# Hedgehog linear attention and a Mish dense layer, twice: averages of two row blocks in one visit, transposes between the row tiles, and the last sums in single banks

## The chip, the core and the metric

The kernel runs on one core of a Trainium2 chip. The core has five engines with an instruction queue each: TensorE (PE; its weight loads are shown apart as PEld), VectorE (DVE), ScalarE (ACT), GpSimd (POOL) and SyncE (SP), which here issues the DMAs. Matmuls write to PSUM, here used as eight banks of 128 partitions x 512 fp32. The metric is the time of the program on the device in microseconds, and lower is better. All engines start together, and the program ends when the last store has landed.

## The reference

Two layers. Each is a linear attention with a learned feature map, followed by a dense layer with the Mish activation; both are behind a layer norm without weights and are added to their input. There are 2048 rows of 640 numbers, 32 heads of 20, and 1536 hidden units.

```python
def _A_ref(x, wqkv, w_phi, wo):
    q, k, v = ...                       # x @ wqkv, split into heads of 20
    pq = jnp.einsum("bhsd,hdf->bhsf", q, w_phi)
    pk = jnp.einsum("bhsd,hdf->bhsf", k, w_phi)
    phi_q = jnp.concatenate([_softmax(pq), _softmax(-pq)], axis=-1)
    phi_k = jnp.concatenate([_softmax(pk), _softmax(-pk)], axis=-1)
    kv = jnp.einsum("bhsf,bhsd->bhfd", phi_k, v)
    z = jnp.einsum("bhsf->bhf", phi_k)
    num = jnp.einsum("bhqf,bhfd->bhqd", phi_q, kv)
    den = jnp.einsum("bhqf,bhf->bhq", phi_q, z)[..., None] + 1e-6
    return (num / den) @ wo             # heads put side by side first

def _B_ref(x, w1, b1, w2):
    h = x @ w1 + b1
    return (h * jnp.tanh(softplus(h))) @ w2

x = A_x
for _ in range(2):
    x = x + _A_ref(_layernorm(x), A_wqkv, A_w_phi, A_wo)
    x = x + _B_ref(_layernorm(x), B_w1, B_b1, B_w2)
```

## The kernel before

**Blocks and stages.** The rows are cut into eight blocks of 256, and a block into two row tiles of 128, called 0 and 1. A layer has three stages, each a loop over the blocks. The first attention stage makes the queries' and keys' features and values, sums `kv` and `z` over all rows, and stores the queries' features, turned, in DRAM (`e_d`). The second attention stage divides, multiplies by `wo`, and adds the rows of x. The dense stage does the rest.

**Products in parts.** A product of fp32 operands is made from three: both operands are split into a high part, which the matmul takes whole, and the low rest, and high x high, high x low and low x high are summed in PSUM. So the product of one row tile with a 640 x 320 half of `wo` (`project_half`, L391) is 5 chunks x 3 = 15 matmuls of 320 columns. This document calls one of them a projection.

**The second attention stage (`attend_second`).** For each block and row tile:

- `load(b)` (L646 to L647) brings a block's query features back from `e_d` in three DMAs: two into `big` tiles (a pool of 5) and one into an `ol` tile (a pool of 6). They are free again when the averages of that block have read them.
- `average(b, t)` (L676) multiplies them by `kvb`, the masked sums of all heads, in 22 matmuls of 63 columns (L686): 11 groups of heads, and two halves of 64 rows. The profile shows each as two instructions, so an average is 44. They use 120 x 64 of the array at a time, where all others here use 128 x 128. The result lies in a pair of PSUM banks, numerator and denominator side by side. VectorE then adds the epsilon (L695, twice), takes the reciprocal (L696) and multiplies, once for each bank (L699). These five instructions are called a division here; `div[0]` is the last of them. The rows come out in a row tile (`xn`, a pool of 4).
- `Transposed(...).all()` turns the two row tiles of a block: ten transposes of 128 x 128 on TensorE (L325) in three groups, each group into a single bank, from which ScalarE makes the high part (through the helper on L134) and VectorE the low part (L331).
- `Rows.half(c, ps)` is 15 projections into a single bank (L714), VectorE's addition of the rows of x (L716) and half of the statistics (L717); `mean` joins them (L721).
- `norm_scale(b, mvs)` makes the layer norm's scale and shift: GpSimd adds the epsilon (L304) and takes the power -1/2 (L305), and VectorE makes the shift from it (L307, once for each row tile).
- The block's rows are stored, and weights of the dense layer that were fetched a block before are split (`makes`, `fetches`).

Meanwhile the first attention stage's last query tile is still being finished: `rest` has its steps (projections, then the reductions L416 and L419 among others, then exp, L425, L426, the product on GpSimd, the turn and the stores), and `tail()` issues one of them, behind the last division.

**Order.** Before: blocks 0 and 1 are averaged ahead of the loop. In pass 1 and pass 2 of the loop, the averages of block 2 and block 3 come first; in passes 2 to 5, blocks 4 to 7 are averaged behind the transposes. So a visit of TensorE to the averages is one block, two averages or 88 instructions. Each visit stands between matmuls of another shape.

**What sets the order of instructions.** The whole program stands in a scheduled block: an engine's instructions are put in order by a simulated timeline, except where a part is written by hand. In the second attention stage the order of TensorE and of SyncE is the program's own (`manual_schedule`); VectorE, ScalarE and GpSimd are ordered by the scheduler, and `issue_after(i)` keeps an instruction behind i. In the dense stage all engines are the scheduler's.

**Banks.** PSUM is two pools: `mm_tile` gives pairs of banks (two pairs), `one_tile` single banks (four). A pool gives its buffers in turn, and the first instruction that writes to a buffer waits for the last that reads what it held. In a pass of the second attention stage the single banks are asked for by four halves and three groups of transposes; the averages ask for pairs.

**The dense stage.** `hidden` (L809) makes 256 hidden units of a block in a single bank (two groups of 128, 15 matmuls of 256 columns each), `mish` the activation, and `contract` (L851), two steps later, adds their part of the output into two pairs of banks, one for each row tile, over six steps. `end` adds the rows of x (L861 in the last block, else L869) and stores them. In the last block of the last layer the four halves are added one by one; the first row tile is stored whole (L865), and the second in two halves (L863). A pair of banks is one tile, so a reader of one bank waits for the last matmul that writes to either.

Of the kernel before, what the change touches and what calls it, by code (L numbers as in the profile page):

```python
# [11 lines left out]
ALU = mybir.AluOpType  # L12
# [32 lines left out]
def kernel(  # L45
# [620 lines left out]
    def attend_second(x_src, x_dst, acc, fetches, makes, fetch_next, begin_next):  # L666
# [9 lines left out]
        def average(b, t):  # L676

            phs = loaded[b]
            po = mm_tile()
            for g in range(G):  # L680
# [3 lines left out]
                for q in range(2):  # L684
                    s0 = t * P + 64 * q
                    nc.tensor.matmul(  # L686
                        po[64 * q:64 * q + 64, c, GW * j:GW * j + w], phs[g][:n, s0:s0 + 64],
                        kvb[:n, g, :w], start=True, stop=True)
            o = row_tile()
            den = work.tile([P, H], F32, tag="r", name="den", bufs=2)  # L690
            pv = [po[:, c, :(DH + 1) * n].rearrange("p (h d) -> p h d", d=DH + 1)
# [32 lines left out]
        with tc.manual_schedule(engines={mybir.EngineType.PE, mybir.EngineType.SP}):  # L724
# [18 lines left out]
            def averages(b):  # L743
                for t in range(BT):
                    average(b, t)
# [5 lines left out]
            for b in range(NB):  # L751
                if b == NB - 1:
                    ahead.all()
                elif b in (1, 2):
                    averages(b + 1)
                r0, r1 = Rows(b, 0), Rows(b, 1)
# [4 lines left out]
                if b in (1, 2):  # L761
                    phi(b + 3)
                if b == NB - 3:
# [5 lines left out]
                if b < 2:  # L769
                    r1.half(0, one_tile())  # L770
                if b + 1 < NB:
                    nxt = Transposed(rows.pop(b + 1)).all()
                if 2 <= b < NB - 2:
                    averages(b + 2)
                    phi(b + 4)
                if b == 2:
                    tail()
                if b >= 2:
                    r1.half(0, one_tile())
                r1.half(1, one_tile())  # L780
                norm_scale(b, [mv0, r1.mean()])
# [13 lines left out]
    def dense(x_src, x_dst, w1s, w2s, first, last):  # L795
# [41 lines left out]
        def contract(b, pr, ah, al):  # L837
            if pr == 0:
                blocks[b][2] = [mm_tile() for _ in range(BT)]
            pys = blocks[b][2]  # L840
            order = [(t, j) for t in range(BT) for j in range(2)]
            if b == NB - 1 and pr == KF // 2 - 1:
                order = [(t, j) for j in range(2) for t in range(BT)]
            for t, j in order:
                sl = slice(t * P, (t + 1) * P)
                f = 2 * pr + j
                for c in range(2):
                    cs = slice(c * HC, (c + 1) * HC)
                    wh, wl = w2s[f][0][:, cs], w2s[f][1][:, cs]
                    for n, (l, r) in enumerate(((ah, wh), (ah, wl), (al, wh))):  # L850
                        nc.tensor.matmul(pys[t][:, c, :HC], l[:, j, sl], r,  # L851
                                         start=(f == 0 and n == 0), stop=(f == KF - 1 and n == 2))
# [170 lines left out]
```

## Time and profile before

| | us |
|---|---|
| three runs | 1362.43, 1364.81, 1365.24; median 1364.81 |
| profiled execution | 1361.69 |
| its span in the profile | 1359.7 |

The profiled execution is one more run, and all rows of the trace are its own. Its TensorE clock was granted at 0.999 of full speed. By stages, with the busy time of the engines in each stretch of the span (us) and the share of time in which the mean DMA engine was busy:

| stretch, us | what | PE | DVE | ACT | POOL | DMA | GB/s |
|---|---|---|---|---|---|---|---|
| 42 to 252 | first attention stage, layer 0 | 210.0 | 178.9 | 89.5 | 104.7 | 0.43 | 93 |
| 252 to 356 | second attention stage, layer 0 | 104.0 | 77.0 | 27.9 | 41.0 | 0.86 | 277 |
| 356 to 690 | dense stage, layer 0 | 334.0 | 270.8 | 170.7 | 79.0 | 0.42 | 109 |
| 690 to 911 | first attention stage, layer 1 | 220.8 | 180.9 | 83.5 | 120.7 | 0.45 | 97 |
| 911 to 1018 | second attention stage, layer 1 | 106.4 | 78.2 | 29.5 | 42.6 | 0.86 | 273 |
| 1018 to 1343 | dense stage, layer 1, without its end | 325.0 | 236.2 | 151.8 | 61.7 | 0.27 | 74 |

In the rows below, L391 is line 391 of the kernel; `one<-r2h,xth` is what is written and what is read, by the program's names. A row of the timeline has the start of a group in us from the start of the span, its length, engine, line, operation, operands with their shapes, and how many instructions it holds; what stands in brackets is idle time before it and what ended it. Rows of the waits give the sum of a wait, its count and the longest. A row of the windows has the stretch, the busy time of PE, PEld, DVE, ACT, POOL (with counts), then the granted clock, the DMA share and GB/s.

### The profile page before, as it was taken

The page shows a single profiled execution, that of the slowest core. Times are in us where ns is not written, and L with a number is a line of the kernel's source. Part 1 is how long each engine was busy: PE and PEld are TensorE (multiplying, and loading weights), DVE is VectorE, ACT ScalarE, POOL GpSimd, SP SyncE. Part 2 cuts the span into 40 slices and gives each one's busy share as a digit, 9 for nine tenths or more (in the row PEclk, how much of TensorE's full clock was granted, in tenths as well). Part 3 has the DMA queues.
Part 4 walks back from the last instruction along what each step waited for, and adds up shares of the span by engine and source line. Part 5 has one row for each costly group of instructions (what it writes and reads, how often), then busy time and mean ns, then how long its engine had stood idle before and what let it go on. Part 6 is the DMA issues. An engine that isn't in the chain of part 4 may idle for free.

```text
span 1359.7 us, 30969 instructions
## 1 busy us (share of the span) xinstructions
PE 1349.6 (99%) x12896; PEld 1338.2 (98%) x12896; DVE 1057.4 (78%) x1799; ACT 576.0 (42%) x967; POOL 464.0 (34%) x417
## 2 busy tenths in 40 slices
PE   9999999999999999999999999999999999999998
PEld 9999999999999999999999999999999999999998
DVE  5888988876687887778769788779668776676775
ACT  4444344322454545445443334332236444444443
POOL 2355644444222222222225555634351211111111
PEclk9999999999999999999999999999999999999999
DMA  9543443797714442244563534559964221233200
GB/s 338 156 103 79 98 96 81 206 287 274 222 40 98 117 117 69 61 106 100 145 209 81 119 79 91 96 120 289 289 246 125 78 72 39 86 98 97 73 26 20
DMA packets 352629, 174.11 MB, mean 128 GB/s; under 512 B 287449, under 2 KB 324041, under 8 KB 352489
## 3 DMA queue, kind: packets, MB, share of 16 engines
q1 hardware_dynamic: 352489, 172.14, 46.7%
q8 instruction: 101, 1.65, 0.5%
q14 instruction: 39, 0.32, 0.1%
HBM read 106.23 MB, written 65.86 MB: 127 GB/s over the span
## 4 chain that ended last, share of the span: by engine, by line
PE 94%; DVE 3%; POOL 1%; ACT 0%; issue 0%; DVEq 0%; POOLq 0%
PE mm L391 25%; PE mm L851 25%; PE one L809 25%; PE one L391 12%; PE mm L686 3%; PE one L325 2%; PE one L464 2%; DVE r L425 1%; DVE m L416 0%; DVE r L419 0%; POOL big L427 0%; DVE big L417 0%; DVE r1l L276 0%; POOL xtl L331 0%; POOL r L427 0%
## 5 line engine op out<-in xcount | busy, mean ns | idle before, releaser
L851 PE MATMUL mm<-r2h,ol 128*128 128x320 f32 x1280 | 304.8, 309 | 0.0
L835 POOL TENSOR_TENSOR ol<-big,ol 128x512 fp32r<-128x512 f32 (+1 forms) x98 | 131.1, 1338 | 477.2 <-ACT ol L834 419.1
L809 PE MATMUL one<-xtl,r1h 128*128 128x256 f32 x960 | 268.2, 279 | 0.0
L809 PE MATMUL one<-xth,r1l 128*128 128x256 f32 x960 | 268.0, 279 | 0.0
L809 PE MATMUL one<-xth,r1h 128*128 128x256 f32 x960 | 265.9, 279 | 0.0
L851 PEld LDWEIGHTS mm<-r2h,ol 128*128 128x128 f32 x1280 | 219.2, 188 | 0.0
L851 PE MATMUL mm<-r2l,ol 128*128 128x320 f32 x640 | 197.3, 309 | 0.0
L391 PE MATMUL mm<-r1h,xth 128*128 128x304 f32 (+1 forms) x600 | 185.1, 309 | 1.5 <-DVE r1l L276 1.5
L391 PE MATMUL mm<-r1l,xth 128*128 128x304 f32 (+1 forms) x600 | 183.8, 306 | 0.0
L391 PE MATMUL mm<-r1h,xtl 128*128 128x304 f32 (+1 forms) x600 | 183.5, 306 | 0.2 <-POOL xtl L331 0.2
L809 PEld LDWEIGHTS one<-xtl,r1h 128*128 128x128 f32 x960 | 180.4, 188 | 0.0
L809 PEld LDWEIGHTS one<-xth,r1l 128*128 128x128 f32 x960 | 180.4, 188 | 0.0
L809 PEld LDWEIGHTS one<-xth,r1h 128*128 128x128 f32 x960 | 179.6, 188 | 0.0
L824 DVE TENSOR_SCALAR big<-big 128x512 f32<-128x512 f32 (+1 forms) x98 | 56.6, 578 | 110.0 <-ACT big L822 109.8
L851 PEld LDWEIGHTS mm<-r2l,ol 128*128 128x128 f32 x640 | 120.2, 188 | 0.0
L834 ACT ACTIVATE ol<-big 128x512 fp32r<-128x512 f32 (+1 forms) x98 | 60.9, 622 | 137.8 <-DVE big L833 137.8
L826 ACT ACTIVATE big<-big,two 128x512 f32<-128x512 f32 (+1 forms) x98 | 70.1, 716 | 116.0 <-DVE big L825 115.9
L822 ACT ACTIVATE big<-one,b1s 128x256 f32<-128x256 f32 x192 | 80.9, 468 | 88.5 <-PE one L809 88.0
L427 POOL TENSOR_TENSOR r<-r,r 128x1280 f32<-128x1280 f32 x32 | 77.2, 2413 | 119.1 <-DVE r L426 101.6
L391 PEld LDWEIGHTS mm<-r1h,xth 128*128 128x128 f32 x600 | 112.8, 188 | 2.6 <-DVE r1l L276 1.7
L391 PEld LDWEIGHTS mm<-r1h,xtl 128*128 128x128 f32 x600 | 112.8, 188 | 0.4 <-POOL xtl L331 0.4
L391 PEld LDWEIGHTS mm<-r1l,xth 128*128 128x128 f32 x600 | 112.8, 188 | 0.1
(142 smaller groups left out, 3118.0 us busy)
## 6 DMA issues: line engine op xcount, KB each, us to landing
e_d<-r SPq DMA_DIRECT2D x128, 160.0 KB, 4.0
big<-e_d SPq DMA_DIRECT2D x32, 640.0 KB, 7.6
x_d<-xt SPq DMA_DIRECT2D x23, 640.0 KB, 3.8
xt<-x_d SPq DMA_DIRECT2D x22, 640.0 KB, 5.5
n_d<-xn SPq DMA_DIRECT2D x168, 80.0 KB, 2.3
xt<-in_x SPq DMA_DIRECT2D x16, 640.0 KB, 4.4
xn<-x_d SPq DMA_DIRECT2D x28, 320.0 KB, 4.4
v<-n_d SPq DMA_DIRECT2D x30, 256.0 KB, 3.1
```

The lines of the kernel that those rows point to most:

```text
L325: nc.tensor.transpose(ps[:, c, t * P:(t + 1) * P], self.rows[t][:, (c0 + c) * P:(c0 + c + 1) * P], ident)
L391: nc.tensor.matmul(ps[:, :w], a[:, sl], r, start=(k == 0 and n == 0), stop=(k == KD - 1 and n == 2))
L427: nc.gpsimd.tensor_tensor(eg, eg, r.unsqueeze(2).to_broadcast([P, 2 * H, DH]), op=ALU.mult)
L464: nc.tensor.matmul(kva[32 * j:32 * j + DH + 1, 40 * r:40 * r + 40], v[:, (DH + 1) * h:(DH + 1) * (h + 1)], e[:, 40 * h:40 * h + 40], start ...
L686: nc.tensor.matmul(po[64 * q:64 * q + 64, c, GW * j:GW * j + w], phs[g][:n, s0:s0 + 64], kvb[:n, g, :w], start=True, stop=True)
L809: nc.tensor.matmul(ph[:, j, :], l, r, start=(n == 0), stop=(n == 3 * KD - 1))
L822: exps[0] = nc.scalar.activation(part(ta, 0)[:, j - js.start], ph[:, j, :], AF.Exp, bias=b1s[:, 2 * pr + j:2 * pr + j + 1]).ins
L824: nc.vector.tensor_scalar_min(e, e, E_CAP)
L826: nc.scalar.activation(r, n, AF.Ln, bias=two)
L834: nc.scalar.activation(ah[:, js], n, AF.Copy)
L835: nc.gpsimd.tensor_tensor(al[:, js], n, ah[:, js].bitcast(F32), op=ALU.subtract)
L851: nc.tensor.matmul(pys[t][:, c, :HC], l[:, j, sl], r, start=(f == 0 and n == 0), stop=(f == KF - 1 and n == 2))
```

## The change

Second attention stage:

- `averages(b)` now does the four averages of blocks b and b+1 in a row. They stand at the start of passes 1, 3 and 5, and there alone: blocks 2 and 3, 4 and 5, 6 and 7. The first two and the fourth have a pair of banks, and the third has two single banks (`single`).
- The loads follow: passes 1 and 3 issue those of two blocks each, 4 and 5, 6 and 7.
- In passes 0, 2 and 4, `norm_scale` is moved to the next pass, behind the averages, and behind their last division by `issue_after(div[0])`.
- The transposes of the next block now always stand between row tile 0 and row tile 1. Before, in passes 0 and 1, the first half of row tile 1 came ahead of them.

End of the last layer:

- In the last block, row tile 1's sums have two single banks in place of a pair, and all four halves are written and read bank by bank.
- The last `contract`'s matmuls have a fixed order, each behind the one before by `issue_after`: row tile 0 first (for both halves the products of the first group of 128 hidden units; then, of the second group, those with the high part of the activation, and last the two with its low part), then row tile 1, six matmuls of one half and six of the other. Before, the first group of hidden units came first, for both row tiles, and then the second.

In every other block the dense stage's sums are in pairs as before. No matmul is added or left out.

```diff
-        def average(b, t):
+        def average(b, t, single=False):
 
             phs = loaded[b]
-            po = mm_tile()
+            if single:
+                po = [one_tile(), one_tile()]
+            else:
+                mm = mm_tile()
+                po = [mm[:, 0], mm[:, 1]]
             for g in range(G):
                 n = 120 if g < 10 else 80
                 w = GW if g < 10 else 42
@@ -684,11 +688,11 @@
                 for q in range(2):
                     s0 = t * P + 64 * q
                     nc.tensor.matmul(
-                        po[64 * q:64 * q + 64, c, GW * j:GW * j + w], phs[g][:n, s0:s0 + 64],
+                        po[c][64 * q:64 * q + 64, GW * j:GW * j + w], phs[g][:n, s0:s0 + 64],
                         kvb[:n, g, :w], start=True, stop=True)
             o = row_tile()
             den = work.tile([P, H], F32, tag="r", name="den", bufs=2)
-            pv = [po[:, c, :(DH + 1) * n].rearrange("p (h d) -> p h d", d=DH + 1)
+            pv = [po[c][:, :(DH + 1) * n].rearrange("p (h d) -> p h d", d=DH + 1)
                   for c, n in ((0, 24), (1, 8))]
             hh = (slice(0, 24), slice(24, H))
             for c in range(2):
@@ -741,8 +745,9 @@
             loaded[3] = load(3)
 
             def averages(b):
-                for t in range(BT):
-                    average(b, t)
+                for n in range(2):
+                    for t in range(BT):
+                        average(b + n, t, (n, t) == (1, 0))
 
             def phi(b):
                 if b < NB:
@@ -751,34 +756,33 @@
             for b in range(NB):
                 if b == NB - 1:
                     ahead.all()
-                elif b in (1, 2):
+                elif b % 2:
                     averages(b + 1)
+                    with tc.issue_after(div[0]):
+                        norm_scale(b - 1, mvs)
                 r0, r1 = Rows(b, 0), Rows(b, 1)
                 r0.half(0, one_tile())
                 tail()
                 if b + 1 < NB:
                     xs[b + 1] = fetch(x_src, b + 1)
-                if b in (1, 2):
+                if b % 2:
                     phi(b + 3)
+                    phi(b + 4)
                 if b == NB - 3:
                     fetch_next()
                 r0.half(1, one_tile())
                 mv0 = r0.mean()
                 if b == NB - 2:
                     ahead = begin_next()
-                if b < 2:
-                    r1.half(0, one_tile())
                 if b + 1 < NB:
                     nxt = Transposed(rows.pop(b + 1)).all()
-                if 2 <= b < NB - 2:
-                    averages(b + 2)
-                    phi(b + 4)
                 if b == 2:
                     tail()
-                if b >= 2:
-                    r1.half(0, one_tile())
+                r1.half(0, one_tile())
                 r1.half(1, one_tile())
-                norm_scale(b, [mv0, r1.mean()])
+                mvs = [mv0, r1.mean()]
+                if b % 2 or b + 2 >= NB:
+                    norm_scale(b, mvs)
                 xt = xs.pop(b)
                 nc.sync.dma_start(row_block(x_dst, b), xt)
                 makes[b]()
@@ -835,21 +839,32 @@
             nc.gpsimd.tensor_tensor(al[:, js], n, ah[:, js].bitcast(F32), op=ALU.subtract)
 
         def contract(b, pr, ah, al):
+            ends = last and b == NB - 1
             if pr == 0:
-                blocks[b][2] = [mm_tile() for _ in range(BT)]
+                if ends:
+                    mm = mm_tile()
+                    blocks[b][2] = [[mm[:, 0], mm[:, 1]], [one_tile(), one_tile()]]
+                else:
+                    blocks[b][2] = [[mm[:, 0], mm[:, 1], mm] for mm in (mm_tile() for _ in range(BT))]
             pys = blocks[b][2]
-            order = [(t, j) for t in range(BT) for j in range(2)]
-            if b == NB - 1 and pr == KF // 2 - 1:
-                order = [(t, j) for j in range(2) for t in range(BT)]
-            for t, j in order:
-                sl = slice(t * P, (t + 1) * P)
+            final = pr == KF // 2 - 1
+            every = range(3)
+            order = [(t, c, j, n) for t in range(BT) for j in range(2) for c in range(2) for n in every]
+            if final and ends:
+                order = [(0, c, 0, n) for c in range(2) for n in every]
+                order += [(0, c, 1, n) for c in range(2) for n in (0, 1)] + [(0, c, 1, 2) for c in range(2)]
+                order += [(1, c, j, n) for c in range(2) for j in range(2) for n in every]
+            elif final and b == NB - 1:
+                order = [(t, c, j, n) for j in range(2) for t in range(BT) for c in range(2) for n in every]
+            before = None
+            for t, c, j, n in order:
                 f = 2 * pr + j
-                for c in range(2):
-                    cs = slice(c * HC, (c + 1) * HC)
-                    wh, wl = w2s[f][0][:, cs], w2s[f][1][:, cs]
-                    for n, (l, r) in enumerate(((ah, wh), (ah, wl), (al, wh))):
-                        nc.tensor.matmul(pys[t][:, c, :HC], l[:, j, sl], r,
-                                         start=(f == 0 and n == 0), stop=(f == KF - 1 and n == 2))
+                w = w2s[f][n == 1][:, c * HC:(c + 1) * HC]
+                with (tc.issue_after(before) if before is not None else nullcontext()):
+                    ins = nc.tensor.matmul(pys[t][c][:, :HC], (ah, ah, al)[n][:, j, t * P:(t + 1) * P], w,
+                                           start=(f == 0 and n == 0), stop=(f == KF - 1 and n == 2))
+                if final and ends:
+                    before = ins.ins
 
         def end(b):
             xt, _, pys = blocks.pop(b)
@@ -858,7 +873,7 @@
                 for t in range(BT):
                     for c in range(2):
                         cs = slice(c * HC, (c + 1) * HC)
-                        nc.vector.tensor_tensor(xt[:, t, cs], pys[t][:, c, :HC], xt[:, t, cs], op=ALU.add)
+                        nc.vector.tensor_tensor(xt[:, t, cs], pys[t][c][:, :HC], xt[:, t, cs], op=ALU.add)
                         if t == BT - 1:
                             nc.sync.dma_start(dst[:, t, cs], xt[:, t, cs])
                     if t < BT - 1:
@@ -866,7 +881,7 @@
                 return
             mvs = []
             for t in range(BT):
-                nc.vector.tensor_tensor(xt[:, t, :].rearrange("p (c d) -> p c d", c=2), pys[t][:, :, :HC],
+                nc.vector.tensor_tensor(xt[:, t, :].rearrange("p (c d) -> p c d", c=2), pys[t][2][:, :, :HC],
                                         xt[:, t, :].rearrange("p (c d) -> p c d", c=2), op=ALU.add)
                 if not last:
                     mvs.append(norm_stats(t, xt))
```

On ScalarE and GpSimd the instructions come in the same order as before. On SyncE only the loads of the query features move; on VectorE and TensorE the order differs in the second attention stage and at the end alone.

More of the change, by code (lines that the diff above doesn't have):

```diff
@@ L1 @@
-from contextlib import ExitStack, contextmanager
+from contextlib import ExitStack, contextmanager, nullcontext
 import concourse.bass as bass
```

## The prediction

> **What bounds the kernel now.** First the page, then the first row of TensorE's waits, longest first:
>
> ```profile
> span 1359.7 us, 30969 instructions
> PE 1349.6 (99%) x12896; PEld 1338.2 (98%) x12896; DVE 1057.4 (78%) x1799; ACT 576.0 (42%) x967; POOL 464.0 (34%) x417
> PE 94%; DVE 3%; POOL 1%; ACT 0%; issue 0%; DVEq 0%; POOLq 0%
> ```
> ```profile
> PE mm L391 <- DVE r1l L276: 1.5, 1, 1.5
> ```
>
> TensorE is busy 99% of the span and is 94% of the chain of waits; its longest wait is 1.5 us, in the folding of the weights (L276) ahead of all this. So only three things can move the time: the spacing of TensorE's matmuls, a new wait of TensorE, and what follows its last matmul. The number of matmuls does not change. The sum is made against the profiled execution, 1361.69 us (span 1359.7 and 2.0 around it), which lies 3.1 below the median of the runs shown, 1364.81; I carry the difference over to the median.
>
> **The change part by part.**
>
> *Averages of two blocks together.* The timeline of TensorE around one pair of averages (L686), and around two groups of transposes, one followed by averages, one by projections:
>
> ```profile
> 930.64 0.31 PE L391 MATMUL one<-r2h,xtl 128*128 128x320 f32 x1
> 930.88 1.38 PE L686 MATMUL mm<-kvb,big 120*64 120x63 f32 x40
> 932.18 1.36 PE L686 MATMUL mm<-kvb,big 120*64 120x63 f32 x40
> 933.57 0.42 PE L391 MATMUL one<-r2h,xth 128*128 128x320 f32 x1
> 933.82 0.31 PE L391 MATMUL one<-r2l,xth 128*128 128x320 f32 x1
> 933.97 0.31 PE L391 MATMUL one<-r2h,xtl 128*128 128x320 f32 x1
> ...
> 976.44 1.25 PE L325 MATMUL one<-ident,xn 128*128 128x128 f32 x10
> 977.62 0.57 PE L686 MATMUL mm<-kvb,big 120*64 120x63 f32 x12
> ...
> 1002.01 1.25 PE L325 MATMUL one<-ident,xn 128*128 128x128 f32 x10
> 1003.02 0.39 PE L391 MATMUL one<-r2h,xth 128*128 128x320 f32 x1
> ```
>
> Projections start 0.147 apart (933.82 to 933.97 and on). The averages start 0.24 after the projection before them, 0.09 too late. The first average takes 930.88 to 932.18, 1.30; the second, up to the next projection, 1.39, 0.09 more; and the first projection then holds the next one back to 0.25, 0.10 too long. A visit to the averages thus costs about 0.29 beside its averages. If the first average's 1.30 contains its own start (some 0.03 for two), a merge is worth 0.33. I take 0.31. The transposes do not act so: followed by projections they take 1.01, and the first projection is 0.08 longer (0.39 for 0.31), 1.09; followed by averages they take 1.18, which is 1.09 and the 0.09 of the entry. Moving them away from the averages is worth 0. Blocks 2 to 7 are six visits before and three after, in each of two layers: 6 x 0.31 = **-1.86** (bounds -1.7 and -2.0).
>
> *Transposes ahead of the second tile's first half, in blocks 0 and 1.* This adds a wait. The single banks rotate through four. In block 0 the new order of allocations is half, half, three transpose groups, half, half; so the sixth, the first half of row tile 1, gets the bank of the second half of row tile 0, and may start when VectorE's addition of that half is done. VectorE's order up to that addition is the old one, and it is late there, since the last query tile's reductions (L416, L425, L419) stand in front:
>
> ```profile
> 259.39 0.42 PE L391 MATMUL one<-r2h,xth 128*128 128x320 f32 x1
> 266.10 1.25 PE L325 MATMUL one<-ident,xn 128*128 128x128 f32 x10
> 927.49 1.25 PE L325 MATMUL one<-ident,xn 128*128 128x128 f32 x10
> ```
> ```profile
> 264.58 0.81 DVE L419 TENSOR_TENSOR r<-m,r 128x640 f32<-128x640 f32 x1
> 265.31 0.48 DVE L716 TENSOR_TENSOR xt<-one,xt 128x320 f32<-128x320 f32 x1
> ...
> 926.44 0.48 DVE L716 TENSOR_TENSOR xt<-one,xt 128x320 f32<-128x320 f32 x1
> 1004.63 1.29 DVE L331 TENSOR_TENSOR xtl<-one,xth 128x512 fp32r<-128x512 f32 x2 [1.16 <-ACT xth L134]
> ```
> ```profile
> 1005.38 0.42 PE L391 MATMUL one<-r2h,xth 128*128 128x320 f32 x1
> ```
>
> Layer 0: the transposes move 15 projections (2.20) earlier, from 266.10 to 263.90, and end 1.01 later, at 264.91. The addition ends at 265.79. The last two rows show the release: in block 6 a half waits for the bank of a low part, two of which run 1004.63 to 1005.92 (the first ends near 1005.3), and TensorE resumes at 1005.38, so about 0.06. TensorE goes on at 265.85: 0.94 late. Layer 1: transposes 925.29 to 926.30, addition done 926.92, TensorE 926.98: 0.68. Together **+1.62**, lower bound 0 (if the bank came free otherwise; a gain is excluded, the same instructions are only reordered), upper 2. Behind TensorE's wait stands the rest of block 0, and so everything.
>
> *Four divisions in a row in block 1.* VectorE now does four instead of two:
>
> ```profile
> 966.52 0.25 DVE L695 TENSOR_SCALAR den<-mm 128x24 f32<-128x24 f32 x2
> ...
> 968.00 0.25 DVE L695 TENSOR_SCALAR den<-mm 128x24 f32<-128x24 f32 x2
> ...
> 936.73 1.48 DVE L425 TENSOR_REDUCE r<-r 128x64 f32<-128x1280 f32 x1
> 938.12 0.48 DVE L716 TENSOR_TENSOR xt<-one,xt 128x320 f32<-128x320 f32 x1
> 938.52 0.54 DVE L426 RECIPROCAL r<-r 128x64 f32<-128x64 f32 x1
> 938.98 0.43 DVE L717 BATCH_NORM_STATS2 bn<-xt 128x6 f32<-128x320 f32 x1
> 978.84 0.23 DVE L307 SCALAR_TENSOR_TENSOR stats<-mv,stats 128x1 f32<-128x1 f32 x2 [3.28 <-POOL stats L305]
> ```
>
> One division is 1.48 (966.52 to 968.00), more than the 1.30 of its average. The fourth average needs the pair of banks of the first division: about 4.0 after the averages start, against a division done at about 3.2, so no wait. Behind the four stand the statistic (L307, 0.15), L425 (1.39 to the next start), the addition (0.40), L426 (0.46), L717 (0.40) and the addition of the second half (0.48): 9.2 in all from the first division. Layer 1: block 0's remaining work on VectorE ends near 933.2, so the addition ends near 942.4. TensorE: from 926.98, two halves (4.5), four averages with entry and exit (5.4), two halves (4.4), transposes (1.0): 942.4. They meet: I take +0.05 in each layer, **+0.10**, bounds 0 and 1.0 a layer.
>
> [...]
>
> *The statistic behind the divisions.* L307 waited 3.28 for GpSimd (last row above) with nothing of TensorE late. Behind the divisions it waits less: 0. If it stood in front, such a wait would reach the fourth average.
>
> *Loads.* Block 5's queries are now loaded with block 4's, a block earlier; 6 and 7 go together in block 3:
>
> ```profile
> 272.00:312.00 40.00, 40.00 (x494) 39.26 (x491) 31.11 (x87) 8.06 (x12) 13.81 (x14) 1.00 1.02 295
> ```
> ```profile
> big<-e_d SPq DMA_DIRECT2D x32, 640.0 KB, 7.6
> 278.00 1.07 SPq L646 DMA_DIRECT2D big<-e_d  x2
> ```
>
> The DMA engines are full there (share 1.02, 295 GB/s). A block's load is 1.36 MB, 4.6 us. Block 4's, issued at 278.0, lands 7.6 later, and block 5's near 291; they are needed near 296 and 298. Of 6 and 7, about 14 us for 4.1 MB with rows and weights issued at 302, the need is at 321. Cost 0; a load that is late costs TensorE as much.
>
> *The last block.* Two of four single banks are held through it, so a hidden result has two to rotate in; the timeline shows them read within 4.5 us of being written, and a turn takes 7: 0. At the end:
>
> ```profile
> 1354.59 1.69 DVE L861 TENSOR_TENSOR xt<-mm,xt 128x320 f32<-128x320 f32 x4 [3.53 <-PE mm L851]
> 1354.83 0.31 PE L851 MATMUL mm<-r2h,ol 128*128 128x320 f32 x1
> 1355.90 0.92 SPq L863 DMA_DIRECT2D out<-xt  x2
> ```
>
> Four additions start when row tile 0 is done, 0.40 apart, the last 1355.79 to 1356.28; its store follows. Now row tile 0 is complete 12 matmuls before the end and the next half 6 before, so only the last addition follows 1355.14: 1355.19 to 1355.68. **-0.60** (bounds -0.5 and -0.65).
>
> Sum: -1.86 + 1.62 + 0.10 - 0.60 = **-0.74**: 1360.95 for the profiled execution, 1364.1 beside the median.
>
> **The rivals.**
> 1. *The block-0 wait does not come* (VectorE or the rotation gives the bank sooner). For it: TensorE waits for nothing here now; against: VectorE's rows there (264.58, 265.31) have no idle time ahead of them, so the addition cannot come sooner. -2.46: 1362.4.
> 2. *Slower: VectorE's chain in blocks 1, 3 and 5 becomes the bound.* Place: the first half of row tile 1, waiting for the addition behind four divisions; the 3.28 of L307 shows how late the statistic can be. It decides from about 0.4 us a layer, where block 1 has no margin. With 1 us in block 1 and 0.5 in 3 and 5, 4 us in both layers: -0.74 + 4 = +3.3, 1368.1.
> 3. *Merging does not save the visit* (the gap belongs to each average, not to the entry). Against: 932.18 follows 930.88 by only 1.30. +1.1: 1365.9.
> 4. *The bunched loads land late.* Against: margins of 5 to 7 us. +5: 1370.
>
> **How the numbers follow.** Chances: forecast 0.52, rival 1 0.15, rival 2 0.20, rival 3 0.08, rival 4 0.05. Alone, the forecast has 1362.5 to 1365.5, by its bounds and the runs' spread. 0.2% is 2.7 us, about what a measurement of this kernel can tell from no change: 1362.1 to 1367.5. Faster: half of rival 1 and a fifth of the forecast, pushed there by that spread, 0.18. Slower: over half of rival 2 and rival 4, 0.16. Same: 0.66. The range, 1361.2 to 1367.6, takes in rival 1, rival 3 and the smaller half of rival 2.
>
> **What would show it.** Right: three visits of 176 averages a layer, each 5.2 to 5.3 from first average to next projection; a wait of TensorE at the first half of row tile 1 in block 0, of 0.9 and 0.7, released by VectorE's L720; none in blocks 3 and 5; the last addition near 0.55 after TensorE's last matmul. Wrong: no such wait, or waits of that line in every odd block; averages waiting for DMA; TensorE idle elsewhere.

## The result and the profile after

| | median of runs, us | ratio to before, with its 95% interval |
|---|---|---|
| before | 1364.09 (1362.34 to 1365.26, 13 runs) | |
| changed | 1361.42 (1360.14 to 1363.05, 13 runs) | 0.9984 (0.9976 to 0.9991) |
| changed, a second time | 1361.71 (11 runs) | 0.9981 (0.9972 to 0.9990) |
| before, run as if it were a change | 1362.70 (12 runs) | 0.9991 (0.9982 to 0.9999) |
| the same again, measured together with the second row of the changed kernel | 1363.13 (11 runs) | 0.9990 (0.9982 to 0.9999) |

The kernel is faster by 0.16%, inside the 0.2% for which the prediction gave 0.66, and inside its range, by 0.2 us at the lower end. The last two rows matter for the size: the unchanged kernel itself reads 0.9990 to 0.9991. By that, about 1.2 us of the 2.7 that the medians show are not the change's; against the control that was measured together with it, the changed kernel is at 1361.71 - 1363.13 = -1.4 us.

The page of the changed kernel, and the line that the change adds to TensorE's waits (total, count, longest). Lines of the changed kernel have other numbers than before: L686 is L690 there, L699 L703, L716 L720, L717 L721, L851 L864, L861 L876, L863 L878 and L865 L880.

```profile
span 1360.3 us, 30985 instructions
PE 1347.8 (99%) x12896; PEld 1336.8 (98%) x12896; DVE 1061.9 (78%) x1799; ACT 575.6 (42%) x967; POOL 462.9 (34%) x417
```
```profile
PE one L391 <- DVE xt L720: 1.4, 2, 0.7
```

This profiled execution (1362.07) is no faster than that of before (1361.69), though the medians are 2.7 apart: one execution each can't be subtracted. So the span is cut at matmuls that both kernels have, and the pieces are compared. In the table each is the distance between two starts of matmuls in the trace (us): up to the first average; from there to the first projection behind the averages of block 1; the loop of blocks, from there to the first hidden matmul; and the end, from the start of the last matmul to the end of the span. The rows "before" and "changed" are the first profiles of the two kernels; the other names are those of the experiments below. The dense stage of layer 0 with the first attention stage of layer 1 (555.9 to 556.1) and the dense stage of layer 1 (337.25 to 337.28) are alike in all.

| profile | start | ahead, layer 0 | loop 0 | ahead, layer 1 | loop 1 | end |
|---|---|---|---|---|---|---|
| before | 252.01 | 7.38 | 96.80 | 8.66 | 96.79 | 4.86 |
| e1_same | 251.57 | 7.38 | 96.79 | 9.22 | 97.10 | 4.86 |
| e9_same | 252.02 | 7.73 | 96.79 | 10.93 | 97.37 | 4.86 |
| changed | 252.37 | 7.66 | 96.78 | 9.63 | 97.00 | 3.69 |
| e10_after | 251.94 | 7.79 | 96.78 | 9.28 | 96.76 | 3.69 |
| e2_end | 251.20 | 8.09 | 97.12 | 8.82 | 96.94 | 3.69 |
| e3_stage | 251.44 | 7.73 | 96.78 | 9.16 | 96.78 | 4.86 |
| e4_order0 | 252.27 | 8.07 | 96.77 | 9.31 | 96.14 | 3.68 |
| e5_bank | 251.88 | 7.50 | 96.08 | 9.27 | 96.08 | 3.69 |
| e6_norm | 251.66 | 7.38 | 100.45 | 9.10 | 99.34 | 3.67 |
| e7_apart | 252.16 | 8.33 | 98.24 | 9.29 | 98.23 | 3.69 |
| e8_both | 251.80 | 7.39 | 95.83 | 9.38 | 95.81 | 3.69 |
| e11_alone | 252.72 | 7.69 | 97.56 | 8.86 | 96.80 | 4.20 |
| e12_late | 251.55 | 9.55 | 95.87 | 11.80 | 97.08 | 3.69 |

Three things are to be seen. The start and the stretches ahead of the loops vary by 1 to 2 us in kernels that have the same instructions there. The loop is 96.8 us before and after, where its shape has changed most. And the end is 1.17 us shorter, alike in every profile of the changed end.

The end of the changed kernel: the additions, the last matmul and the stores, and last the first store of before:

```profile
1355.19 0.89 DVE L876 TENSOR_TENSOR xt<-mm,xt 128x320 f32<-128x320 f32 x2 [2.36 <-PE mm L864]
...
1356.95 0.49 DVE L876 TENSOR_TENSOR xt<-one,xt 128x320 f32<-128x320 f32 x1 [0.39 <-PE one L864]
```
```profile
1356.60 0.31 PE L864 MATMUL one<-r2h,ol 128*128 128x320 f32 x1
```
```profile
1356.11 0.34 SPq L880 DMA_DIRECT2D out<-xt  x1
1356.59 1.21 SPq L878 DMA_DIRECT2D out<-xt  x2
```
```profile
1355.51 0.34 SPq L865 DMA_DIRECT2D out<-xt  x1
```

The last addition ends 0.84 behind the start of the last matmul (before 1.45). The first store, with half of the bytes, is issued 0.50 ahead of that matmul, before 0.68 behind it.

The visit of four averages in block 1 of the changed kernel, on TensorE's timeline (start, length, engine, line, operation, tiles, count):

```profile
270.84 0.31 PE L391 MATMUL one<-r2h,xtl 128*128 128x320 f32 x1
271.08 1.39 PE L690 MATMUL mm<-kvb,big 120*64 120x63 f32 x40
...
272.39 1.36 PE L690 MATMUL mm<-kvb,big 120*64 120x63 f32 x40
...
273.67 1.36 PE L690 MATMUL one<-kvb,big 120*64 120x63 f32 x40
...
274.95 1.36 PE L690 MATMUL mm<-kvb,big 120*64 120x63 f32 x40
...
276.35 0.42 PE L391 MATMUL one<-r2h,xth 128*128 128x320 f32 x1
276.60 0.31 PE L391 MATMUL one<-r2l,xth 128*128 128x320 f32 x1
```

From the first average to the projection behind it 5.27; the entry (0.24 for 0.147) and the exit (0.25 behind the first projection) come once. Block 0 of layer 0, TensorE and VectorE:

```profile
264.53 1.26 PE L325 MATMUL one<-ident,xn 128*128 128x128 f32 x10
266.48 0.41 PE L391 MATMUL one<-r2h,xth 128*128 128x320 f32 x1 [0.69 <-DVE xt L720]
265.21 0.81 DVE L419 TENSOR_TENSOR r<-m,r 128x640 f32<-128x640 f32 x1
265.94 0.48 DVE L720 TENSOR_TENSOR xt<-one,xt 128x320 f32<-128x320 f32 x1
```

The transposes start 4.51 us into the loop, where the prediction put them (263.90 - 259.39), and the half behind them starts 0.06 after the addition of the half before (266.42). The waits' view counts 0.69 of it, from the end of a row, and rows overlap (projections are 0.31 long and start 0.147 apart); by starts, 0.965 from the last transpose to the projection, where 0.029 is usual: 0.94 lost. Layer 1 has 0.964.

### The profile page after: what moved, and what is told of

Its sections match the earlier page's. It is cut to its first block, busy times and chain, and to the rows that moved or that the text cites. A ratio compares the mean times of both kernels' runs of the same rounds, so it can differ in the third digit from the quotient of the medians.

```text
span 1360.3 us, 30985 instructions
## 1 busy us (share of the span) xinstructions
PE 1347.8 (99%) x12896; PEld 1336.8 (98%) x12896; DVE 1061.9 (78%) x1799; ACT 575.6 (42%) x967; POOL 462.9 (34%) x417
## 4 chain that ended last, share of the span: by engine, by line
PE 91%; DVE 4%; DMA 1%; POOL 1%; issue 0%; ACT 0%; SPq 0%; DVEq 0%; POOLq 0%
PE one L813 25%; PE mm L391 25%; PE mm L864 24%; PE one L391 11%; PE mm L690 2%; PE one L325 2%; PE one L464 1%; DVE r L425 1%; PE one L864 1%; DVE m L416 1%; DMA ol<-e_d 1%; PE one L690 1%; DVE r L419 1%; POOL big L427 0%; DMA big<-e_d 0%
## 5 line engine op out<-in xcount | busy, mean ns | idle before, releaser
L864 PE MATMUL mm<-r2h,ol 128*128 128x320 f32 x1240 | 296.1, 309 | 0.0
L864 PEld LDWEIGHTS mm<-r2h,ol 128*128 128x128 f32 x1240 | 212.4, 188 | 0.0
L864 PE MATMUL mm<-r2l,ol 128*128 128x320 f32 x620 | 191.2, 309 | 0.0
L864 PEld LDWEIGHTS mm<-r2l,ol 128*128 128x128 f32 x620 | 116.5, 188 | 0.0
```

Of the source, the lines that this page charges most:

```text
L864: ins = nc.tensor.matmul(pys[t][c][:, :HC], (ah, ah, al)[n][:, j, t * P:(t + 1) * P], w, start=(f == 0 and n == 0), stop=(f == KF - 1 and ...
```

## The experiments

**Control: before, unchanged, twice (e1_same, e9_same).** No edit.

> The kernel before, unchanged, as a control and for a second profile. If the matmuls' spacing is fixed and only starts and DMA waits vary, its ratio to itself is 1.000 within 0.001, the loop of blocks from the first projection after the averages of block 1 to the end of the stage is again 96.8 us in both layers, and the stretch ahead of it (8.65 us in layer 1, 7.6 in layer 0) is where it differs from the first profile, by waits of the averages for their loads. Rival: the first profile of before is typical, and every stretch repeats within 0.1 us; then the 2.4 us by which it lies below its median is outside the span.

Ratio 0.9991 (0.9982 to 0.9999). Layer 0 repeats to 0.01; in layer 1 the stretch ahead is 0.56 longer and the loop 0.31. So the ratio comes out 0.001 below 1 for the same kernel, if only just beyond its interval, and the loop of before is not fixed: something in it waits at times.

> The kernel before, unchanged, a second time as a control beside the changed kernel. The traces so far give the changed kernel 1.2 us (its end), and the waits for weights and loads vary from run to run by as much. Theory: the control again reads below 1 (the first did, 0.9991), so that part of the changed kernel's 0.9984 is the comparison's own. Rival: the first control was chance, this one reads 1.000.

Ratio 0.9990 (0.9982 to 0.9999): both controls read alike. What makes the ratio do so isn't settled. Its loop in layer 1 is 0.58 over 96.79.

**The changed kernel again (e10_after).** No edit.

> The changed kernel, a second time, beside the control. Theory: 1.2 to 1.5 us below the control (the end 1.17, and the waits for GpSimd's statistic of 0.2 to 0.3 us that profiles of the old order show in block 4), that is 0.9990 of it. Rival: the 2.7 us of the medians hold against the control too, 0.9980 of it, and a gain is missing from the account.

1.4 us below the control (1361.71 and 1363.13), by the two ratios 0.9981 / 0.9990 = 0.9991, 1.2 us. The theory holds, the rival falls: no gain of the size of 2.7 us is missing.

**The end alone (e2_end).** Before, with the diff's part from `contract` on (single banks for row tile 1, the order of the last matmuls, `end`).

```diff
-                blocks[b][2] = [mm_tile() for _ in range(BT)]
+                    blocks[b][2] = [[mm[:, 0], mm[:, 1]], [one_tile(), one_tile()]]
...
+                order += [(1, c, j, n) for c in range(2) for j in range(2) for n in every]
```

> Only the end of the last layer is changed, the second attention stage is that of before. Theory: from the start of the last matmul to the end of the span 3.70 us, where before has 4.87, so -1.17: -0.61 from the last addition and -0.56 from its store, which lands alone. Rival: the store's 0.56 was chance, and the change is the -0.60 of the prediction. Ratio 0.9991 or 0.9996.

The end is 3.69 for 4.86, -1.17 as in the changed kernel; 1361.55 us, 1.15 below the control that was measured together with it (e1_same, 1362.70); ratio 0.9985 (0.9976 to 0.9993), 0.9994 of the control's.

**The stage alone (e3_stage).** The changed kernel's `attend_second` with the end of before.

```diff
-                blocks[b][2] = [[mm[:, 0], mm[:, 1]], [one_tile(), one_tile()]]
+                blocks[b][2] = [mm_tile() for _ in range(BT)]
...
```

> Only the second attention stage is changed, the end is that of before. Theory (each visit saved is 0.3, each block 0 waits 0.94): loop of blocks in each layer within 0.1 us of before's 96.8 us, the whole ratio 1.000; TensorE's waits for the addition on L720 again two, of 0.9 each. Rival: the stage gives the greater part of the gain that the medians show, by fewer waits for loads: ratio 0.9985 or less.

Both loops are 96.78, with two waits for L720 of 0.94. The time, 1361.87, is 0.83 below the same control (0.9988, 0.9980 to 0.9997, for 0.9991), within what the intervals leave open. The theory of the loops is right; whether the stage gains a little can't be told from the time, only from what follows.

**Where the loop of before waits at times.** All of the excess over 96.79 stands in one place, the first half of row tile 1 in block 4. The control e9_same, layer 1, TensorE, GpSimd and VectorE:

```profile
982.75 0.27 PE L686 MATMUL mm<-kvb,ol 80*64 80x42 f32 x4
983.52 0.42 PE L391 MATMUL one<-r2h,xth 128*128 128x320 f32 x1 [0.51 <-DVE xt L716]
```
```profile
977.88 3.49 POOL L164 TENSOR_TENSOR r1l<-raw,r1h 128x1536 fp32r<-128x1536 f32 x1 [9.25 <-ACT r1h L134]
981.72 0.69 POOL L305 TENSOR_TENSOR stats<-ve,neg_half 128x2 f32<-128x2 f32 x1
```
```profile
982.45 0.23 DVE L307 SCALAR_TENSOR_TENSOR stats<-mv,stats 128x1 f32<-128x1 f32 x2 [3.27 <-POOL stats L305]
...
983.00 0.47 DVE L716 TENSOR_TENSOR xt<-one,xt 128x320 f32<-128x320 f32 x1
```

It reads backwards: TensorE waits for an addition, VectorE's addition stands behind L307, L307 waits for GpSimd's power, and that stands behind the split of a part of w1 (L164), which had to wait for its weights (9.25 for ScalarE's part, L134; in the profile of before that waits 7.04 for the DMA). When those come is set on SyncE's queue. First the control, then the second profile of the changed kernel, both in layer 1 (start and length of issue):

```profile
957.80 2.23 SPq L646 DMA_DIRECT2D big<-e_d  x2
...
960.69 2.01 SPq L646 DMA_DIRECT2D big<-e_d  x2
...
965.01 3.55 SPq L783 DMA_DIRECT2D x_d<-xt  x1
968.66 0.38 SPq L156 DMA_DIRECT2D raw<-in_w  x1
```
```profile
958.79 0.65 SPq L787 DMA_DIRECT2D x_d<-xt  x1
959.54 0.83 SPq L156 DMA_DIRECT2D raw<-in_w  x1
```
```profile
971.27 3.52 POOL L164 TENSOR_TENSOR r1l<-raw,r1h 128x1536 fp32r<-128x1536 f32 x1 [1.10 <-ACT r1h L134]
975.14 0.69 POOL L305 TENSOR_TENSOR stats<-ve,neg_half 128x2 f32<-128x2 f32 x1
```

Before, pass 2 issues the loads of blocks 5 and 6, and the weights stand behind both. The changed kernel has no load in pass 2. From the loop's start (923.41 and 921.76) the weights are issued at 45.2 and 37.8, and the power ends at 59.0 and 54.1. In the ten loops that have the old order of loads:

| end of block 3's power, us from the loop's start | 57.07 | 57.12 | 57.51 | 58.02 | 58.40 | 58.56 | 58.73 | 58.76 | 59.00 | 59.19 |
|---|---|---|---|---|---|---|---|---|---|---|
| loop over 96.79 | 0.00 | 0.00 | 0.01 | 0.00 | 0.01 | 0.15 | 0.31 | 0.33 | 0.58 | 0.77 |

Above 58.4 every bit of lateness goes into the loop. The mean is 0.22 a loop, 0.43 a run. In the six loops of the changed order of loads and of all else in the stage (the changed kernel twice, e3_stage) the power ends at 54.08 to 54.64, and none has a wait at this place (the 0.22 in loop 1 of the changed kernel's first profile is one spacing of 0.364 between two projections, for which the trace names no cause). No kernel with the old loads alone was run, so that the loads do it rests on the queue's rows, not on an experiment. The new visits make the place no easier: with one block's averages fewer ahead of it, TensorE comes to that half 56.98 us into the loop, before 59.54, so the power has to end that much sooner.

**The old order in block 0 (e4_order0).**

```diff
+                if b == 0:
+                    r1.half(0, one_tile())
                 if b + 1 < NB:
                     nxt = Transposed(rows.pop(b + 1)).all()
...
-                r1.half(0, one_tile())
+                if b > 0:
+                    r1.half(0, one_tile())
```

> The changed kernel, with the first half of row tile 1 ahead of the transposes in block 0 alone, as before. Theory: the two waits of 0.94 us vanish and nothing takes their place, so the loop of blocks is 95.85 us in each layer and the time 1.88 us below the changed kernel: ratio to before 0.9970. Rival: the wait moves on, since VectorE is late anyway and the second half of row tile 1 or the averages of block 1 wait for the same chain: no gain, loop 96.8 us, ratio 0.9984.

The two waits are gone, but the loops are 96.14 in layer 1 and 96.77 in layer 0, not 95.85. In both, 0.30 came back in block 1, at the same half: VectorE is as late as before, and TensorE now comes sooner. In layer 0 a further 0.60 came back in block 4, by the chain above (power at 55.83, and TensorE 0.63 sooner there). So the rival is right in part. Ratio 0.9976 (0.9966 to 0.9985), 2.04 below the control e1_same, 0.87 of it beside the end.

**Another bank for that half in block 0 (e5_bank).**

```diff
-                r1.half(0, one_tile())
+                r1.half(0, mm_tile()[:, 0] if b == 0 else one_tile())
```

> The changed kernel, with the transposes ahead of both halves of row tile 1 as in it, but the first half of row tile 1 of block 0 in a bank of a pair. Theory (the single bank of the half before is what it waits for): the wait behind the transposes of block 0 is gone, with VectorE as late as ever; TensorE then comes to block 1 by 0.94 us sooner and meets VectorE there, as it did with the old order (0.31 us at the first half of row tile 1): loop of blocks 96.15 us a layer for 96.78. Rival: the half waits for the transposes' own results or for VectorE in another way, and the 0.94 us stay: 96.78.

Both loops are 96.08: the wait of 0.94 is gone with the order of the matmuls unchanged, so it was the bank, and 0.23 came back in block 1. Ratio 0.9973 (0.9962 to 0.9984).

**The statistic not behind the divisions (e6_norm).**

```diff
                     averages(b + 1)
-                    with tc.issue_after(div[0]):
-                        norm_scale(b - 1, mvs)
...
-                if b % 2 or b + 2 >= NB:
-                    norm_scale(b, mvs)
+                norm_scale(b, mvs)
```

> The changed kernel, with each block's statistic issued at that block's end again, not behind the divisions. VectorE then has L307 inside the first of the four divisions. From the profile of the changed kernel GpSimd's power ends at 301.37 and 963.69 in pass 3 where that division is half done at 298.5 and 960.8, and at 327.19 and 990.69 in pass 5 (half done 323.7 and 986.3), since GpSimd first splits a weight part for 3.5 us or more. Theory: the fourth average waits for the pair of banks of the first division: about 2.0 us late in pass 3 and 2.5 in pass 5, nothing in pass 1, some 4.5 us a layer: loop 101.3 us, ratio to before 1.005. Rival: the wait is made good by TensorE's own slack on that side (VectorE is idle later in the pass): under 0.5 us a layer, ratio 0.999.

Ratio 1.0036 (1.0023 to 1.0048), loops 100.45 and 99.34, so 3.7 and 2.6 lost for 4.5 each. In pass 3 of layer 0, GpSimd, VectorE and TensorE:

```profile
300.01 0.69 POOL L305 TENSOR_TENSOR stats<-ve,neg_half 128x2 f32<-128x2 f32 x1
```
```profile
297.56 0.66 DVE L703 TENSOR_TENSOR xn<-mm,den 128x480 f32<-128x480 f32 x1
300.74 0.23 DVE L307 SCALAR_TENSOR_TENSOR stats<-mv,stats 128x1 f32<-128x1 f32 x2 [2.52 <-POOL stats L305]
300.88 0.32 DVE L703 TENSOR_TENSOR xn<-mm,den 128x160 f32<-128x160 f32 x1
```
```profile
301.35 1.49 PE L690 MATMUL mm<-kvb,big 120*64 120x63 f32 x40 [1.95 <-DVE xn L703]
```

The fourth average waits for the first division, which has L307 in its middle. In layer 1 passes 3 and 5 lose 1.16 and 1.34; in layer 0 pass 3 loses 2.1 so, and pass 5 nothing. The other 1.5 of layer 0 is the clock, granted at 0.50 there (below).

**The visits apart again (e7_apart).**

```diff
-                    averages(b + 1)
+                    averages(b + 1, (0,))
...
                 r0.half(0, one_tile())
+                if b % 2 and b < NB - 1:
+                    averages(b + 1, (1,))
```

> The changed kernel, with the averages of the second block of each visit put behind the first half of row tile 0: six visits a layer for three, all else alike. Theory (0.31 us for each visit saved): loop of blocks 0.93 us longer, 97.7 us a layer, and TensorE's first average after a projection again 0.24 behind it. Rival: the gap belongs to each average and not to the visit: loop unchanged at 96.78 us.

Loops 98.24 and 98.23, 1.45 over 96.78. A wait in block 1 has 0.45 of it (0.479 from the transposes to the next projection, for 0.029); the rest, 1.0, is three more visits, 0.33 each. The rival falls. Ratio 1.0007 (0.9998 to 1.0016).

**Both mends (e8_both).**

```diff
-                r1.half(0, one_tile())
+                r1.half(0, mm_tile()[:, 0] if b < 2 else one_tile())
...
                     nxt = Transposed(rows.pop(b + 1)).all()
+                if b and b % 2 == 0:
+                    with tc.issue_after(last_low[0]):
+                        norm_scale(b - 1, mvs)
...
-                if b % 2 or b + 2 >= NB:
+                if b + 2 >= NB:
                     norm_scale(b, mvs)
```

> The changed kernel, with the first half of row tile 1 of blocks 0 and 1 in a bank of a pair, and the statistics of blocks 1, 3 and 5 issued behind the low parts of the next block's transposes. Theory: no wait of TensorE for an addition is left, in either block, nor the one in block 4 that the profile of the old order in block 0 shows (0.6 us, when GpSimd's statistic is late): loop 95.85 us in both layers, time 1.9 us below the changed kernel and 3 below before; ratio 0.9970 or less. Rival: VectorE is late by itself in block 1 and some other wait takes their place: loop 96.2 or more.

Loops 95.83 and 95.81; median 1359.44, ratio 0.9967 (0.9955 to 0.9979), 2.0 to 2.3 below the changed kernel's two medians. TensorE in block 0 of layer 0:

```profile
263.70 1.26 PE L325 MATMUL one<-ident,xn 128*128 128x128 f32 x10
264.71 0.39 PE L391 MATMUL mm<-r2h,xth 128*128 128x320 f32 x1
```

1.01 from the transposes to the half, as the prediction has it for transposes that nothing follows late. This is the fastest version.

**The store alone (e11_alone).** Before, with two of the last block's three stores left out.

```diff
-                        if t == BT - 1:
+                        if t == BT - 1 and c == 1:
                             nc.sync.dma_start(dst[:, t, cs], xt[:, t, cs])
-                    if t < BT - 1:
-                        nc.sync.dma_start(dst[:, t], xt[:, t])
```

> The kernel before without two stores of the last block of the last layer: row tile 0 and the first half of row tile 1 are not stored, so their rows of the output are left as they were. Theory (the last store is late in landing because it shares the DMA engines with the two ahead of it): its time from issue to landing falls from 2.26 us to the changed kernel's 1.8, and its issue comes 0.05 earlier after the addition. Rival: 2.26 us is what a store of this size takes here, and 1.8 another chance of it.

The last addition ends at 1358.26 and the store is issued at 1358.29 (0.03; before 1356.28 and 1356.36, 0.08). The transfers' view from then on, first before and then without the two others (count, size, us from issue to landing):

```profile
out<-xt SPq DMA_DIRECT2D x1, 160.0 KB, 2.3
```
```profile
out<-xt SPq DMA_DIRECT2D x1, 160.0 KB, 1.8
```

To the hundredth 2.26 and 1.78. The theory holds, and the rival falls: the last store takes 2.25 to 2.26 in the four profiles that have the old end with all stores, and 1.80 to 1.82 in the nine that have the new one. But the changed kernel's last store is not alone either: issued at 1357.47, it takes 1.81, while the two ahead of it land only at 1358.29 and 1358.76. They were issued 1.36 and 0.88 ahead of it (before 0.86 and 0.46), and more of their data has moved by then: from the last store's issue on the transfers' view has 0.46 MB, before 0.64. From the issue of the first store to the landing of the last it is 3.11 before and 3.17 after; what moved against the last matmul is the first store, by 1.17.

**Four stores behind a load (e12_late).** The version with both mends, and block 6's first query tile stored behind the load of block 1.

```diff
+            if i == NT - BT - 1:
+                late.append((e, dst[t]))
+                return
...
             loaded[1] = load(1)
+            for e, to in late:
+                for q in range(4):
+                    nc.sync.dma_start(to[q], e[32 * q:32 * q + 32].rearrange("f (j s) -> f j s", s=32))
```

> As the version with both mends (pair banks, statistics behind the low parts), and the four stores of one query tile (block 6's first) issued behind the load of block 1, ahead of which they stand now. Theory: the averages ahead of the loop wait for that load because the stores keep the DMA engines until the load's data can start; without them ahead it lands 2 us sooner, and the stretch ahead of the loop falls from 9.4 to about 8 us in layer 1 and to 7.4 in layer 0: 1.5 us below that version, ratio 0.9955. Rival: the last query tile, which takes over the buffer that these stores read, comes late in turn, and VectorE's chain in block 0 with it: the loop grows by as much as the stretch ahead of it shrinks.

The averages no longer wait for a load, but the stretches ahead of the loops grew, from 7.39 and 9.38 to 9.55 and 11.80; ratio 0.9993 (0.9984 to 1.0002). (Loop 1, 97.08, holds projections at a granted clock of 0.50, below.) ScalarE and TensorE ahead of the loop of layer 1:

```profile
921.12 0.74 ACT L134 ACTIVATE r<-one 128x304 f32<-128x304 f32 x2 [7.84 <-DMA e_d<-r]
```
```profile
921.59 0.69 PE L325 MATMUL one<-ident,xn 128*128 128x128 f32 x2 [2.85 <-ACT r L134]
```

The rival has the cause right, but not the place: the last query tile waits for the stores' buffer, so its single bank is still unread when the transposes ahead of the loop need it, and loop 0 stays at 95.87.

## Why the prediction was right, and what it had wrong

- **A visit, 0.31.** Right: 0.33 in e7_apart, and (96.79 - 95.82) / 3 = 0.32 in e8_both, where no wait covers it. Six visits saved, -1.9 for -1.86.
- **Block 0, +0.94 and +0.68.** Right in place, cause and releaser; e5_bank shows that it is the bank. Layer 1 was mis-sized: in the profile of before VectorE's addition stood 0.26 sooner against TensorE there than in layer 0. Four of the five profiles with the old stage have such a lead in layer 1, and none with the new one has; why is not shown. The changed kernel waits 0.94 in both. +1.88 for +1.62: it gives back all that the visits save.
- **Block 1, +0.10 in all.** Nothing came. "They meet" was right: in layer 1 of the changed kernel the addition ends at 944.03, and the half starts at 944.16; in e5_bank, where TensorE comes 0.94 sooner, 0.23 is lost there.
- **The statistic, 0.** Right, and the sentence on what it would cost in front is shown by e6_norm: 3.7 and 2.6 us.
- **Loads, 0.** Wrong. The prediction asked only whether the bunched loads would be late. It did not ask what stands behind the loads that leave pass 2: the weights, GpSimd's split, block 3's power, L307, an addition. That is worth 0.43 a run by the ten loops, and the profile of before, in which the power ended at 57.51 and 58.02, just missed showing it.
- **The end, -0.60.** The addition is right (last matmul to the end of the last addition 1.45 and 0.84, -0.61). The step that failed is the one left out, the stores: that row tile 0 is done, and stored, sooner leaves less data to move when the last store is issued (0.46 MB for 0.64). That store lands in 1.81 for 2.26, another 0.45; 0.05 is saved to its issue, and some 0.06 between its landing and the end of the span (1.01 for 1.07). -1.17.
- **The sum.** -1.9 + 1.9 - 0.4 - 1.2 = -1.6 for -0.74, against -1.4 to the control. The predicted 1364.1 lies 2.7 above the median of 1361.42: 0.9 of that is this account; the rest is the anchor, since the three runs of before that were shown (1364.81) stood above all thirteen (1364.09), and whatever makes the same kernel read 1.2 us low, by its ratio of 0.9991. That the median still lies in the range, 0.2 us from its end, is partly luck; by the time alone it is nearer to rival 1 (1362.4), and only the traces tell the two apart.
- **The rivals.** 1: the wait came; its -2.46 also left out that block 1 takes some of it back, 0.23 a layer in e5_bank. 2: no wait for VectorE in blocks 1, 3 and 5. A division takes VectorE longer than its average takes TensorE (1.48 and 1.30 in the profile of before), but TensorE does not wait for it in those blocks, as long as VectorE has nothing else to wait for: in e6_norm a wait of 2.52 us inside the first division holds TensorE up by 2.1. 3: fell with e7_apart. 4: no average of the loop waited for a load.

## What to carry to other kernels

Gathering work of another shape into fewer visits is worth what the entry and exit cost, times the visits (0.33 us each here); but a new order of allocations can give it all back where a buffer's turn comes on a late reader (0.94 a layer here), and taking one buffer from another pool mended that here without a new order (loops of 96.08 for 96.78). When a transfer is moved, look also at what it no longer stands in front of. At the end of a kernel count the stores as well as the last addition: here the last one landed in 1.81 us for 2.26, with 0.46 MB for 0.64 left to move at its issue, so finish and store a part early. And where single executions differ by more than the change, cut the traces at common instructions, and run the unchanged kernel as a control.

## What the runs showed of the hardware

TensorE's granted clock was 0.50 at three single waits: 1.95 us in layer 0 of e6_norm, 1.8 in layer 1 of e9_same (a spacing of 1.97) and 2.85 in layer 1 of e12_late (a spacing of 3.13). The windows of e6_norm behind the wait of 1.95 us above (stretch, busy times, then clock, DMA share, GB/s):

```profile
302.00:303.00 1.00, 1.00 (x30) 0.92 (x26) 0.96 (x5) 0.00 (x0) 0.00 (x0) 0.74 1.05 395
303.00:304.00 1.00, 1.00 (x5) 1.00 (x5) 0.97 (x3) 0.00 (x0) 0.00 (x0) 0.50 0.98 400
304.00:305.00 1.00, 1.00 (x6) 1.00 (x5) 0.93 (x5) 0.00 (x0) 0.00 (x0) 0.50 1.10 340
305.00:306.00 1.00, 1.00 (x6) 1.00 (x6) 0.62 (x2) 0.00 (x0) 0.00 (x0) 0.55 1.06 205
```

Nine projections were 0.267 apart for 0.147; with the end of the averages and the first projection behind them, 1.5 us were lost, over half of the wait itself on top of it. By an estimate from the clocks of the windows (a us at 0.50 counts whole, at 0.74 as 0.52), it was halved for 3.4 us in e6_norm (0.52 + 2.00 + 0.90) and in e9_same (0.48 + 2.00 + 0.92), and for 6.8 us in e12_late (1.28 + 5.00 + 0.56). After a spacing of 2.23 in layer 0 of e12_late, and after 1.43 in the changed kernel, the clock stayed at 1.00. So the length of the wait alone does not tell which ones it followed, and no run here shows what does.
